# Pooled attention into two MLPs on one core: where weight stores and fetches stand in the order, and the opening of the first block

## The chip, the core and the metric

One core of one Trainium2 chip. The metric is the device time of one execution in microseconds (us). The kernel before took 2052.91 us (median of 3 runs, 2050.61 to 2057.3). TensorE (PE) multiplies, VectorE (DVE), ScalarE (ACT) and GpSimd (POOL) work elementwise, SyncE (SP) issues all the DMAs of this kernel, in program order.

## The reference, cut to what matters

```python
# q, k, v: 8 batches, 8 heads, 576 positions, 64 wide
k_p = k.reshape(B, H, 72, 8, 64).mean(axis=3)       # v_p likewise
scores = (1/8) * q @ k_p^T ;  scores -= max
attn = exp(scores) ; attn /= sum + 1e-9
x = (attn @ v_p) as 4608 tokens x 512
x = (sigmoid(x @ w_gate) * (x @ w_val)) @ w_out     # 512 -> 1536 -> 512
h = x @ w_in                                        # 512 -> 2048
y = where(h > 0, h, exp(min(h, 0)) - 1) @ w_out     # 2048 -> 512
```

The weights come as 64-bit floats, in DRAM read as pairs of 32-bit integers. Each is narrowed to one 32-bit float by four VectorE operations on integers and then kept as two reduced-precision halves, high and low, so that a product is three matmuls (high x high, high x low, low x high).

## The kernel before, in words

**Stages.** The 4608 tokens go in nine blocks of 512, n = 0 to 8. A prelude (0 to 69 us in the profile) does the attention of block 0 and the first conversions of weights. Blocks 0 and 1 (69 to 229, 229 to 376) run the gated MLP plainly, in twelve steps c over the 1536 columns, while the 36 pieces of w_gate, w_val and w_out are converted (block 0, `convert`) and sums of weights are formed and stored (block 1, `form_weights`). Blocks 2 to 8 (376 to 1282) multiply by a Strassen-like scheme: twelve units u, each of seven products k. The second MLP runs from 1282 to 2050.

**What goes on behind the products.** During block n the attention of block n+1 is worked out, at places (u, k) of a table (`thin_plan`, with Q_AT, S_AT, T_AT). The previous block's output is flushed (`flush_one`, L631 and L638) at u = 0. Also the second MLP's weights are converted by the generator `prepared` (L252 on): 16 pieces of w_in, two and two as a pair, then 16 of w_out. For each there is a fetch to a raw tile (`rw`, L124 or L130), a `magnitude` on ScalarE (L268), four VectorE operations (`narrow_1`, `narrow_2`: L105, L109, L115, L119), differences (L305 to L310), a split in halves (ScalarE L273, GpSimd L277) and a store (`wd`, `wod`, L278). `work()` advances the generator by one step, at the places that WORK_AT names for even and odd u.

**What sets the order.** Each engine runs its instructions in program order; the Python order of the calls is that order. The raw tiles have two buffers in rotation, so a fetch waits until the store that last read its buffer has landed. The tiles `rq`, `rkv`, `yo` share rotating row buffers. SP issues in order too: an issue that waits for its data or its buffer holds up every issue behind it. In the prelude a score tile (`ats`, L482), the exponent, the norm (L513 to L521) and the transposes (`att`, L528) follow tile by tile, and `emit_pv` (L552, L559) multiplies by the values.

Of the kernel before, what the change touches and what calls it, by code (L numbers as in the profile page):

```python
# [24 lines left out]
def fused_kernel(  # L25
# [41 lines left out]
    ps = ctx.enter_context(tc.tile_pool(name="ps", bufs=1, space=PSUM))  # L67
# [137 lines left out]
    def convert(n, ahead=2, peek=1):  # L205

        for _ in range(n):
            i = count["one"]
# [18 lines left out]
    def form_weights(cc, i):  # L227


        wa, wb = wg[2 * cc], wg[2 * cc + 1]  # L230
        ra, rb = plain_t().bitcast(F32), plain_t().bitcast(F32)
        lo, hi = slice(0, HW), slice(HW, NW)
        sub = ALU.subtract
        for r, w in ((ra, wa), (rb, wb)):
            nc.vector.tensor_tensor(out=r, in0=f32(flat(w[:, i, 0])), in1=f32(flat(w[:, i, 1])), op=ALU.add)
            yield
        nc.vector.tensor_tensor(out=ra[:, lo], in0=rb[:, lo], in1=ra[:, lo], op=sub)
        nc.vector.tensor_tensor(out=rb[:, lo], in0=rb[:, hi], in1=rb[:, lo], op=sub)
        yield
        split(flat(wb[:, i, 0, 0:SQ]), flat(wb[:, i, 1, 0:SQ]), ra[:, lo])  # L240
        nc.vector.tensor_tensor(out=rb[:, hi], in0=rb[:, hi], in1=ra[:, lo], op=sub)
        nc.vector.tensor_tensor(out=ra[:, hi], in0=rb[:, hi], in1=ra[:, hi], op=sub)
        yield
        two = raw_tile("t32").rearrange("p f w -> p (f w)").rearrange("p (m s f) -> p m s f", m=2, s=2).bitcast(F32R)
        one = plain_t().rearrange("p (s f) -> p s f", s=2).bitcast(F32R)
        split(two[:, :, 0], two[:, :, 1], rb.rearrange("p (m f) -> p m f", m=2))
        nc.sync.dma_start(out=t_dram[2 * cc + i][:, 0:2], in_=f32(two))
        yield
        split(one[:, 0], one[:, 1], ra[:, hi])
        nc.sync.dma_start(out=t_dram[2 * cc + i][:, 2], in_=f32(one))  # L250
        yield

    def prepared():
# [16 lines left out]
        def upper(r, src):  # L270
            d = r.rearrange("p f w -> p (f w)").rearrange("p (s f) -> p s f", s=2).bitcast(F32R)
            d = d[:, :, :src.shape[1]]
            nc.scalar.activation(out=d[:, 0], in_=src, func=AF.Copy)  # L273
            return d

        def lower(d, src, place):
            nc.gpsimd.tensor_tensor(out=d[:, 1], in0=src, in1=f32(d[:, 0]), op=ALU.subtract)  # L277
            nc.sync.dma_start(out=place, in_=f32(d))  # L278

        def both(place, src):  # L280
            d = upper(raw_tile("rs2"), src)
            lower(d, src, place)

        def narrowed(i):
            for half in (narrow_1(tiles[i]), narrow_2(raws[i], tiles[i])):
                for _ in half:
                    yield
# [4 lines left out]

        fetch(0)
        yield
        magnitude(0)
        yield
        for i in range(len(loads)):
            q, second = divmod(i, 2)
            yield from narrowed(i)
            t, r = tiles[i].bitcast(F32), raws[i]  # L300
            if i < C2 and second:
                a, b = tiles.pop(i - 1).bitcast(F32), t
                c = plain_t().bitcast(F32)
                lo, hi = slice(0, 256), slice(256, 512)
                nc.vector.tensor_tensor(out=c[:, hi], in0=b[:, hi], in1=b[:, lo], op=ALU.subtract)  # L305
                nc.vector.tensor_tensor(out=b[:, lo], in0=b[:, lo], in1=a[:, lo], op=ALU.subtract)
                lower(upper(r, t), t, part(q, 1))
                yield
                nc.vector.tensor_tensor(out=c[:, lo], in0=b[:, hi], in1=b[:, lo], op=ALU.subtract)
                nc.vector.tensor_tensor(out=a[:, hi], in0=c[:, lo], in1=a[:, hi], op=ALU.subtract)  # L310
                yield
                both(part(q, 2), c)
                yield
                both(part(q, 3, 1), a[:, hi])
                fetch(i + 1)
                yield
            else:
                d = upper(r, t)
                fetch(i + 1)
                lower(d, t, part(q, second) if i < C2 else wo2_dram[i - C2])  # L320
                yield
            magnitude(i + 1)
            yield

    def background():
        for cc in range(C1 // 2):
            for i in range(2):
                while formed[0] <= cc:
                    yield
                yield from form_weights(cc, i)  # L330
        yield from prepared()

    formed = [0]
# [12 lines left out]
    ps_at = wide.enter_context(tc.tile_pool(name="ps_at", bufs=1, space=PSUM))  # L346
# [76 lines left out]
    def emit_k(b):  # L423

        a = ps_at.tile([P, 2, 512], F32, name="atk", tag="at")
# [40 lines left out]
    def emit_q(t, d=None):  # L466
        r = q_raw.pop(t)
        if d is None:
            a = ps_at.tile([P, 2, 512], F32, name="atq", tag="at")[:, 0, :]
            d = q_tile()  # L470
        else:
            a = ps.tile([P, 512], F32, name="atq0", tag="acc", bufs=4)
# [16 lines left out]
    def off_peak(p, a, n):  # L489
# [3 lines left out]
        mx = at_p.tile([P, n, H // 2], F32, name="mx", tag="mx")  # L493
# [6 lines left out]
    def emit_s(t, p=None):  # L500
        a = ps_at.tile([P, 2, 512], F32, name="ats", tag="at")
        scores(a, t, range(HP), q_t.pop(t))
        p = p_tile() if p is None else p
# [6 lines left out]
    def emit_norm(t, p):  # L510
        p3 = p.rearrange("p (h k) -> p h k", k=SP)
        sm = at_p.tile([P, H], F32, name="sm", tag="sm")
# [3 lines left out]
        pl = at_p.tile([P, HP, WIN], F32, name="pl", tag="pl")  # L516
# [18 lines left out]
    def emit_t(t, spare=False):  # L535
        if spare:
            a = [ps.tile([P, 512], F32, name="att0", tag="acc", bufs=4) for _ in range(2)]
        else:
            both = ps_at.tile([P, 2, 512], F32, name="att", tag="at")
            a = [both[:, 0, :], both[:, 1, :]]  # L540
# [25 lines left out]
    def emit_pv(n):  # L566

        a = ps_at.tile([P, 2, 512], F32, name="atv", tag="at")
        d = [a[:, 0, :], a[:, 1, :]] + [ps.tile([P, NW], F32, name="xv", tag="gv", bufs=2) for _ in range(2)]
# [79 lines left out]
    Q_AT = (1, 4, 7, 9)  # L649
    S_AT = (2, 5, 8, 10)  # L650
    T_AT = (3, 6, 9, 11)
# [23 lines left out]
    with tc.manual_schedule():  # L675
# [38 lines left out]
        qt = spare("qt0")  # L714
        convert(1, 0, 0)
        for c in range(NCH):
            pool_k(0, c)
        emit_k(0)
        open_to(2)
        for i in range(TPW):  # L720
            emit_q(i, qt[:, i])
        convert(1, 0, 0)
        room = [spare("p0"), spare("p1")]
        room = [r.rearrange("p a n -> p (a n)") for r in room]
        ph = [room[t // 3][:, t % 3 * HK:(t % 3 + 1) * HK] for t in range(TPW)]

        def between(t):

            if t == 0:
                convert(1, 1, 0)  # L730
            elif t == 1:
                for c in range(NCH):
                    pool_v(0, c)
            elif t == 2:
# [654 lines left out]
```

## Time and profile before

| | us |
|---|---|
| median of 3 runs | 2052.91 |
| profiled execution, its own time | 2051.42 |
| its span (first to last instruction) | 2049.7 |
| PE busy | 1825.4 (89%) |
| DVE busy | 1099.1 (54%) |
| ACT busy | 854.8 (42%) |
| POOL busy | 631.2 (31%) |
| chain that ended last | PE 63%, DVE 15%, DMA 8%, ACT 5% |

A busy PE is not PE at full speed: the granted clock (PEclk, in shares of 2.4 GHz) has two levels, 1.2 and 2.4 GHz, and a stretch between them shows a mean below 1. Idle time of PE is the stretch less its busy time.

### The profile page before, as it was taken

Reading aid. Unit: us, or ns where it says so; the run is one execution under the profiler, and the core shown is the slowest. Engines: PE = TensorE matmul, PEld = TensorE weight load, DVE = VectorE, ACT = ScalarE, POOL = GpSimd, SP = SyncE. Lnnn points to the kernel's source line nnn. Section 1 sums busy time; section 2 is a strip of 40 time slices with the busy share of each in tenths; the row PEclk is TensorE's granted clock in tenths of the full one; section 3 lists DMA queues with packets and bytes.
Section 4 is the critical chain, followed back from the end, with each engine's and each line's share of the span. In section 5 each row is a group of like instructions: output and inputs, shape, how many; then the busy total and the mean of one; then the engine's idle time right before and its main releaser. Section 6 shows DMA issues by size and latency. Waiting matters only on the chain.

```text
span 2049.7 us, 27976 instructions
## 1 busy us (share of the span) xinstructions
PE 1825.4 (89%) x10212; PEld 1612.1 (79%) x10212; DVE 1099.1 (54%) x2073; ACT 854.8 (42%) x1727; POOL 631.2 (31%) x635
## 2 busy tenths in 40 slices
PE   3577888698889888988999979999999999999999
PEld 2456766587778877877888869899999999999898
DVE  6689455565555655646656546344434444344432
ACT  3344333343344343433434423444444454444443
POOL 2245244332333232323333322222222222222222
PEclk7698998899999998999999989999999999999999
DMA  6454233655654755656656586634334343343521
GB/s 169 129 172 146 96 128 118 211 175 187 210 195 160 235 189 185 198 180 224 197 197 216 175 325 238 246 118 169 110 138 174 108 172 138 117 165 111 189 110 50
DMA packets 150906, 346.82 MB, mean 169 GB/s; under 512 B 47728, under 2 KB 79472, under 8 KB 150768
## 3 DMA queue, kind: packets, MB, share of 16 engines
q1 hardware_dynamic: 150768, 345.02, 49.4%
q8 instruction: 81, 1.33, 0.3%
q14 instruction: 57, 0.47, 0.1%
HBM read 287.31 MB, written 57.67 MB: 168 GB/s over the span
## 4 chain that ended last, share of the span: by engine, by line
PE 63%; DVE 15%; DMA 8%; ACT 5%; issue 4%; SPq 2%; POOL 2%; ACTq 0%; DVEq 0%; POOLq 0%
PE oacc L1266 19%; PE bank L1220 17%; PE pl L1105 12%; PE acc L606 8%; DMA rw<-in_moe_w_out_dram 2%; PE gv L581 2%; DMA wd<-rs 2%; DMA rw<-in_moe_w_in_dram 1%; DVE sg L1142 1%; PE ats L482 1%; DVE vs L438 1%; SPq L638 1%; DMA rkv<-in_k_dram 1%; DMA rkv<-in_v_dram 1%; DVE sm L513 1%
## 5 line engine op out<-in xcount | busy, mean ns | idle before, releaser
L1220 PE MATMUL bank<-form,wr 128*128 128x384 f32 x2016 | 411.0, 338 | 1.0 <-DVE u L1253 0.7
L1220 PEld LDWEIGHTS bank<-form,wr 128*128 128x128 f32 x2016 | 366.5, 188 | 29.1 <-DVE u L1253 1.1
L606 PE MATMUL acc<-g,wos 128*128 128x512 f32 x1152 | 353.8, 403 | 1.3 <-ACT g L92 1.2
L1266 PE MATMUL oacc<-w2o,gc 128*128 128x512 f32 x1080 | 288.9, 393 | 0.4 <-POOL gc L93 0.4
L1266 PEld LDWEIGHTS oacc<-w2o,gc 128*128 128x128 f32 x1080 | 199.6, 187 | 30.4 <-POOL gc L93 0.8
L606 PEld LDWEIGHTS acc<-g,wos 128*128 128x128 f32 x1152 | 195.2, 194 | 15.0 <-ACT g L92 1.7
L93 POOL TENSOR_TENSOR g<-sg,g 128x512 fp32r<-128x512 f32 x108 | 141.2, 1315 | 174.5 <-ACT g L92 172.1
L1105 PE MATMUL pl<-s,wg 128*128 128x256 f32 x1008 | 159.2, 296 | 37.3 <-DVE u L1120 20.0
L93 POOL TENSOR_TENSOR gc<-ea,gc 128x384 fp32r<-128x384 f32 x96 | 98.1, 1022 | 298.1 <-ACT gc L92 295.0
L1105 PEld LDWEIGHTS pl<-s,wg 128*128 128x128 f32 x1008 | 144.6, 197 | 55.9 <-DVE u L1120 29.5
L1105 PE MATMUL pl<-s,tt 128*128 128x256 f32 x1008 | 163.9, 302 | 22.7 <-DVE sg L1132 17.6
L93 POOL TENSOR_TENSOR gc<-pair,gc 128x384 fp32r<-128x384 f32 x96 | 98.1, 1022 | 260.7 <-ACT gc L92 240.2
L1105 PEld LDWEIGHTS pl<-s,tt 128*128 128x128 f32 x1008 | 148.5, 204 | 34.9 <-DVE sg L1132 18.8
L1105 PE MATMUL pl<-a,wg 128*128 128x256 f32 x1008 | 157.2, 294 | 5.9 <-ACT sg L1127 5.8
L1105 PEld LDWEIGHTS pl<-a,wg 128*128 128x128 f32 x1008 | 146.3, 199 | 16.5 <-ACT sg L1127 6.8
L581 PE MATMUL gv<-x,wg 128*128 128x512 f32 x576 | 150.3, 416 | 8.2 <-DVE sg L599 4.4
L1266 PE MATMUL oacc<-w2p,gc 128*128 128x512 f32 x540 | 143.1, 393 | 0.0
L581 PEld LDWEIGHTS gv<-x,wg 128*128 128x128 f32 x576 | 113.6, 201 | 34.6 <-issue 6.2
L92 ACT ACTIVATE g<-sg 128x512 fp32r<-128x512 f32 x108 | 67.8, 628 | 168.5 <-DVE sg L1142 121.2
L1266 PEld LDWEIGHTS oacc<-w2p,gc 128*128 128x128 f32 x540 | 99.8, 187 | 14.8
L528 PE MATMUL att<-ident,p 128*128 128x128 f32 x144 | 27.9, 326 | 87.5 <-POOL p L521 68.7
L277 POOL TENSOR_TENSOR rw<-nt,rw 128x512 fp32r<-128x512 f32 x32 | 43.6, 1364 | 176.0 <-ACT rw L273 176.0
(199 smaller groups left out, 2841.4 us busy)
## 6 DMA issues: line engine op xcount, KB each, us to landing
wr<-wd SPq DMA_DIRECT2D x96, 896.0 KB, 6.4
tt<-td SPq DMA_DIRECT2D x84, 768.0 KB, 4.7
wos<-wd SPq DMA_DIRECT2D x96, 512.0 KB, 5.7
rw<-in_moe_w_out_dram SPq DMA_DIRECT2D x22, 512.0 KB, 4.3
r<-yd SPq DMA_DIRECT2D x24, 384.0 KB, 7.8
out_dram<-po SPq DMA_DIRECT2D x36, 256.0 KB, 2.0
rw<-in_moe_w_in_dram SPq DMA_DIRECT2D x16, 512.0 KB, 6.2
wd<-rw SPq DMA_DIRECT2D x16, 512.0 KB, 3.5
```

Of the source, the lines that this page charges most:

```text
L92: nc.scalar.activation(out=dst_hi, in_=src, func=AF.Copy)
L93: eng.tensor_tensor(out=dst_lo, in0=src, in1=f32(dst_hi), op=ALU.subtract)
L277: nc.gpsimd.tensor_tensor(out=d[:, 1], in0=src, in1=f32(d[:, 0]), op=ALU.subtract)
L438: nc.vector.tensor_reduce(out=t, in_=r.rearrange("p (r d) -> p d r", r=POOL), op=ALU.add, axis=AX.X)
L482: nc.tensor.matmul(a[o:o + n, i // 2, (i % 2) * w:(i % 2 + 1) * w], lhsT=qt[:, j * P + o:j * P + o + n], rhs=kbd[b % 2][:, j * w:(j + 1) * w],
L513: nc.vector.tensor_reduce(out=sm, in_=p3, op=ALU.add, axis=AX.X)
L528: nc.tensor.transpose(a[:, (c % HP) * P:(c % HP + 1) * P], src, ident)
L581: nc.tensor.matmul(d, lhsT=w[:, i, a_w, j], rhs=x[j][:, a_x], start=(j == 0 and a_w == 0 and a_x == 0), stop=(j == KD - 1 and a_w == 1),)
L606: return lambda: nc.tensor.matmul(acc[m], lhsT=w[:, a_w, m * P:(m + 1) * P], rhs=g[:, a_g], start=(c == 0 and a_w == 0 and a_g == 0), stop ...
L1105: nc.tensor.matmul(src, lhsT=w(a_w, j), rhs=f_t[nm][:, j, a_x], start=opens and m == 0, stop=m == 5, skip_group_check=True,)
L1220: nc.tensor.matmul(bank[b ^ flip], lhsT=wp[q][a_w][:, w, j * P:(j + 1) * P], rhs=form_tile(s, a)[j][:, a_x], start=opens and n == 0, stop= ...
L1266: return lambda: nc.tensor.matmul(acc[t + i], lhsT=g[c][:, a_g, i * P:(i + 1) * P], rhs=wo2[2 * q + e][a_w], start=opens and p == 0, stop= ...
```

## The change

No arithmetic is added or taken away. Eight things move:

- `halves`: the store of a converted w_out piece is issued two conversions later (`stores`).
- `form_weights`: the two stores of a unit's sums wait until the third step of the next unit.
- `prepared`: two fetches ahead at the start; a pair takes 17 steps (15 before); each store is issued at least a step after its split; the fetch of the next piece stands three steps ahead of its magnitude, the one after that about six; w_out pieces take six steps, with the fetch three steps ahead (one before).
- WORK_AT, MORE_AT, LAST_AT: 34 steps in a block, which are two pairs; other places.
- the flush at k = 1, 2, 3, 6 of u = 0 (2 to 5 before).
- attention tables: queries at u = 1, 3, 5, 7, scores at 2, 4, 6, 8, transposes at 4, 6, 8, 10; the norm one product earlier; two steps of the keys one product earlier.
- block 1: seven `work` steps per c, three of them in the middle (six at the end before).
- the prelude: PSUM tiles of two banks in four buffers; the scores of tiles 0 to 3 close together, norms and transposes behind; five conversions ahead of `emit_pv(0)` and one behind (six ahead before).

```diff
+    stores = []
     def halves(dst, then=None):
...
             if then:
-                then()
+                stores.append([2, then])
...
+    for q in range(C2 // 2):                      # prepared, one pair
...
+            de = halved(raws[i], tiles[i].bitcast(F32))
+            magnitude(i + 1)
+            yield
+            steps = narrowing(i + 1)
+            next(steps)
+            yield
+            store(de, part(q, 0))
+            yield from steps
...
+            dc = halved(raw_tile("rs2"), c)
+            yield
+            store(do, part(q, 1))
+            yield
+            store(dc, part(q, 2))
+            da = halved(raw_tile("rs2"), a[:, hi])
+            yield
+            fetch(i + 2)
+            yield
+            store(da, part(q, 3, 1))
+            yield
+            yield
+            magnitude(i + 2)
+            fetch(i + 3)
+            yield
...
-        WORK_AT = ((2, 3, 4, 6), (2,))
+        WORK_AT = ((0, 3, 4), (2, 3))
+        FLUSH_AT = (1, 2, 3, 6)
+        MORE_AT = {(0, 5), (1, 4), (10, 1), (11, 1)}
...
         convert(1, 0, 0)
...
+        scored(0)
         convert(1, 0, 0)
...
+        scored(1)
+        scored(2)
+        emit_norm(0, ph[0])
+        scored(3)
...
+        emit_pv(0)
         convert(1)
-        emit_t(TPW - 1, True)
-        convert(1)
-        emit_pv(0)
```

What SP issues in units 7 to 9 of block 3 of the kernel before (`tt`: the sums for the products, `wos`: w_out of the first MLP, `rkv`, `rq`: rows of keys, values and queries, `wd<-`: stores of prepared weights, `rw<-`: fetches):

```order
L278 DMA wd_109<-rw_4312 256x1x512
L392 DMA rkv<-in_v_dram 128x1x512
L278 DMA wd_109<-rs_4673 256x1x512
L810 DMA tt<-td_91 128x1536
L621 DMA wos_4699<-wd_101 128x1024
L278 DMA wd_109<-rs_4710 256x1x256
L124 DMA rw_4714<-in_moe_w_in_dram 128x4x256
L362 DMA rq<-in_q_dram 128x8x64
L810 DMA tt<-td_92 128x1536
L621 DMA wos_4808<-wd_102 128x1024
```

What SP issues from where the fetches of block 3 now stand:

```order
L305 DMA wd_108<-rs_4206 256x1x512
L126 DMA rw_4319<-in_moe_w_in_dram 128x4x256
L445 DMA rkv<-in_v_dram 128x512
L868 DMA tt<-td_88 128x1536
L673 DMA wos_4362<-wd_98 128x1024
L305 DMA wd_108<-rs_4299 256x1x256
L445 DMA rkv<-in_v_dram 128x512
L126 DMA rw_4445<-in_moe_w_in_dram 128x4x256
L868 DMA tt<-td_89 128x1536
L445 DMA rkv<-in_v_dram 128x512
L673 DMA wos_4469<-wd_99 128x1024
L415 DMA rq<-in_q_dram 128x8x64
```

The fetch stood right behind the last store of its pair, and `rq` and the `tt` of the next unit behind it. Now the two fetches stand units earlier, each with a unit's `tt` and `wos` behind it, and no fetch is left at the old place.

What SP issues at the start of block 4 before (`yd`: the previous block's flushed output):

```order
L278 DMA wd_110<-rw_4955 256x1x512
L638 DMA yd_75<-yo 128x384
L638 DMA yd_76<-yo 128x128
L638 DMA yd_75<-yo 128x384
L638 DMA yd_76<-yo 128x128
L278 DMA wd_110<-rs_5347 256x1x512
L638 DMA yd_75<-yo 128x384
L638 DMA yd_76<-yo 128x128
L810 DMA tt<-td_85 128x1536
L638 DMA yd_75<-yo 128x384
L638 DMA yd_76<-yo 128x128
L390 DMA rkv<-in_k_dram 128x512 x2
```

and of the change:

```order
L690 DMA yd_75<-yo 128x384
L690 DMA yd_76<-yo 128x128
L690 DMA yd_75<-yo 128x384
L690 DMA yd_76<-yo 128x128
L690 DMA yd_75<-yo 128x384
L690 DMA yd_76<-yo 128x128
L868 DMA tt<-td_85 128x1536
L443 DMA rkv<-in_k_dram 128x512 x2
L690 DMA yd_75<-yo 128x384
L690 DMA yd_76<-yo 128x128
L415 DMA rq<-in_q_dram 128x8x64
L305 DMA wd_110<-rw_5023 256x1x512
```

The store of prepared weights ahead of the flushes and the one between them are gone from there, and the first two `rkv` rows of keys come ahead of the last flush, while `rq` stands between the second and third row of keys.

What PE does in the prelude before, from the last tile of queries on (`atq`: queries transposed, `ats`: scores, `att`: probabilities transposed, `atv`, `xv`: product with the values):

```order
L474 MATMUL atq_235<-ident,q_143 128x128 x4
L482 MATMUL ats<-kbd_137,qt_187 128x144 x8
L528 MATMUL att_306<-ident,p_245 128x128 x4
L528 MATMUL att_307<-ident,pl 128x128
L482 MATMUL ats<-kbd_137,qt_187 128x144 x4
L528 MATMUL att_343<-ident,p_245 128x128 x4
L528 MATMUL att_344<-ident,pl 128x128
L482 MATMUL ats<-kbd_137,qt_187 128x144 x4
```

and of the change:

```order
L524 MATMUL atq<-ident,q_140 128x128 x16
L532 MATMUL ats<-kbd_134,qt_184 128x144 x16
L578 MATMUL att<-ident,p_185 128x128 x4
L578 MATMUL att<-ident,pl 128x128
L578 MATMUL att<-ident,p_185 128x128 x4
```

All 16 score products are now one row in the program, and the transposes of the four tiles follow one another with no score between.

## Rows read from the trace of the kernel before

**Rows 1.** Stretches by stage: us, busy of each engine, granted clock, DMA.

```profile
0.00:69.00 69.00, 24.43 (x97) 18.79 (x97) 40.02 (x66) 21.36 (x47) 17.10 (x33) 0.73 0.62 168
69.00:229.00 160.00, 123.09 (x550) 97.97 (x551) 134.43 (x179) 74.05 (x130) 75.31 (x58) 0.89 0.44 142
229.00:376.00 147.00, 124.54 (x565) 102.03 (x564) 80.02 (x125) 54.15 (x102) 58.37 (x60) 0.92 0.37 122
376.00:521.00 145.00, 118.26 (x780) 105.03 (x779) 84.18 (x179) 55.09 (x116) 45.76 (x50) 0.92 0.58 191
521.00:927.00 406.00, 350.91 (x2318) 315.25 (x2317) 237.46 (x511) 159.02 (x335) 128.76 (x139) 0.92 0.59 194
927.00:1053.00 126.00, 115.11 (x778) 101.86 (x777) 78.21 (x168) 52.97 (x112) 42.01 (x46) 0.97 0.65 210
1053.00:1167.00 114.00, 109.09 (x740) 97.38 (x739) 68.27 (x153) 49.76 (x97) 34.93 (x33) 1.00 0.61 202
1167.00:1282.00 115.00, 97.38 (x627) 88.37 (x625) 62.52 (x133) 33.66 (x76) 30.09 (x27) 0.91 0.74 268
1282.00:2050.00 768.00, 762.63 (x3769) 685.42 (x3768) 313.99 (x566) 354.76 (x719) 198.85 (x194) 1.00 0.38 141
```

**Rows 2.** Waits of the whole span: us in total, times, longest.

```profile
...
POOL rw L277 <- ACT rw L273: 176.0, 30, 12.7
...
ACT nt L268 <- DMA rw<-in_moe_w_in_dram: 50.3, 8, 9.7
```

**Rows 3.** Timeline, block n=3: start, us, engine, line, [idle before <- releaser].

```profile
...
594.15 0.52 SPq L278 DMA_DIRECT2D wd<-rs  x1
...
602.00 0.38 SPq L124 DMA_DIRECT2D rw<-in_moe_w_in_dram  x1
...
607.12 0.66 ACT L268 ACTIVATE nt<-rw 128x512 f32<-128x512 f32 x1 [9.40 <-DMA rw<-in_moe_w_in_dram]
...
609.93 1.11 PE L528 MATMUL att<-ident,p 128*128 128x128 f32 x4 [7.87 <-POOL p L521]
```

**Rows 4.** Stretches right behind two stalls, columns as in Rows 1.

```profile
609.90:617.00 7.10, 7.07 (x35) 6.51 (x36) 4.71 (x11) 2.56 (x6) 3.99 (x5) 0.64 0.06 21
667.80:674.60 6.80, 5.63 (x24) 5.13 (x24) 1.19 (x3) 1.21 (x3) 0.73 (x1) 0.61 0.99 325
```

**Rows 5.** Timeline, start of block n=4: TensorE.

```profile
...
667.83 1.65 PE L1105 MATMUL pl<-s,tt 128*128 128x256 f32 x6 [4.05 <-DVE sg L1132]
...
675.64 0.98 PE L1105 MATMUL pl<-s,wg 128*128 128x256 f32 x6 [2.15 <-DVE u L1136]
```

**Rows 6.** Waits of block n=8 (1167 to 1282).

```profile
...
ACT nt L268 <- DMA rw<-in_moe_w_out_dram: 28.8, 5, 10.3
```

**Rows 7.** Waits of block n=1 (229 to 376).

```profile
...
PE atq L474 <- DMA rq<-in_q_dram: 13.2, 2, 7.4
```

**Rows 8.** Timeline, end of the prelude.

```profile
...
52.09 0.34 SPq L175 DMA_DIRECT2D wd<-wo  x1
52.53 0.38 SPq L130 DMA_DIRECT2D rw<-in_moe_w_out_dram  x1
...
57.85 0.66 ACT L199 ACTIVATE nt<-rw 128x512 f32<-128x512 f32 x1 [8.84 <-DMA rw<-in_moe_w_out_dram]
...
59.04 3.23 PE L552 MATMUL atv<-pt,vbd 128*128 128x512 f32 x6 [7.00 <-ACT pt L92]
```

**Rows 9.** VectorE by line, block n=0: form, count, busy, mean ns.

```profile
...
L105 DVE TENSOR_SCALAR nt<-nt 128x512 f32<-128x512 f32 x22 | 19.8, 899 | 2.5 <-ACT nt L199 2.5
```

**Rows 10.** Timeline, prelude: one operation alone, and beside GpSimd.

```profile
...
40.35 0.68 DVE L119 SCALAR_TENSOR_TENSOR nt<-rwo,nt 128x512 int32<-128x512 int32 x1
...
50.62 1.44 POOL L93 TENSOR_TENSOR wo<-nt,wo 128x512 fp32r<-128x512 f32 x1
...
50.87 1.75 DVE L119 SCALAR_TENSOR_TENSOR ntr<-rw,ntr 128x512 int32<-128x512 int32 x1
```

**Rows 11.** DMA issues: count, KB each, median us to landing.

```profile
...
tt<-td SPq DMA_DIRECT2D x84, 768.0 KB, 4.7
```

More of the change, by code (lines that the diff above doesn't have):

```diff
@@ L207, in convert @@
         for _ in range(n):
+            for x in stores:
+                x[0] -= 1
+            while stores and stores[0][0] <= 0:
+                stores.pop(0)[1]()
             i = count["one"]
@@ L268, in magnitude, with halved, store, narrowing @@
                 nc.scalar.activation(out=tiles[i].bitcast(F32), in_=raws[i][:, :, 1].bitcast(F32), func=AF.Abs)
[L270 removed]
+        def halved(r, src):
             d = r.rearrange("p f w -> p (f w)").rearrange("p (s f) -> p s f", s=2).bitcast(F32R)
             d = d[:, :, :src.shape[1]]
[L273 removed]
+            split(d[:, 0], d[:, 1], src)
             return d
[L276 to L277 removed]
+        def store(d, place):
             nc.sync.dma_start(out=place, in_=f32(d))
[L280 to L284, printed above, removed]
+        def narrowing(i):
             for half in (narrow_1(tiles[i]), narrow_2(raws[i], tiles[i])):
[L286 to L287 removed]
+                yield from half
                 yield
@@ L291, in part @@
             return w_dram[q][:, :, 2 * n:2 * n + m].rearrange("p s a f -> p s (a f)")
+        sub = ALU.subtract
+        lo, hi = slice(0, 256), slice(256, 512)
         fetch(0)
-        yield
+        fetch(1)
+        for _ in range(3):
+            yield
         magnitude(0)
         yield
[L297 to L321, printed above, removed]
@@ new lines, in prepared @@
+        last = None
+        for i in range(C2, len(loads)):
+            steps = narrowing(i)
+            next(steps)
+            if last is not None:
+                store(last, wo2_dram[i - 1 - C2])
+            yield
+            next(steps)
+            yield
+            next(steps)
+            if last is not None:
+                fetch(i + 1)
+            yield
+            yield from steps
+            last = halved(raws[i], tiles[i].bitcast(F32))
+            yield
+            magnitude(i + 1)
+            yield
@@ L331, in background @@
+        yield
+        yield
+        store(last, wo2_dram[C2 - 1])
+    def background():
+        yield from form_weights()
         yield from prepared()
-    formed = [0]
     working = background()
@@ L423, in emit_k @@
     def emit_k(b):
[L425 removed]
+        a = two_banks("atk")
         flat = a.rearrange("p a n -> p (a n)")
@@ L533, in keep_p, with emit_t @@
         split(hi, lo, a[:, 0:(c1 - c0) * P].rearrange("p (c n) -> p c n", n=P), nc.vector)
[L535 to L540, printed above, removed]
+    def emit_t(t):
+        both = two_banks("att")
+        a = [both[:, 0, :], both[:, 1, :]]
         for c in range(NCH):
@@ L714, in fused_kernel, with scored @@
         qt = spare("qt0")
+        room = [spare("p0"), spare("p1")]
+        room = [r.rearrange("p a n -> p (a n)") for r in room]
+        ph = [room[t // 3][:, t % 3 * HK:(t % 3 + 1) * HK] for t in range(TPW)]
+        def scored(t):
+            emit_s(t, ph[t])
+            emit_exp(ph[t])
         convert(1, 0, 0)
```

178 lines of the change are left out of this document (102 added, 76 removed).

## The prediction

> **What bounds the kernel now.** I read the stretches by stage first, then the waits, then the timeline at the longest waits. In the stretches [rows 1] the reader is to see that the second MLP is no place for a gain: 762.6 of its 768 us are PE's, at full clock. Before it PE idles: 44.6 us of the prelude's 69, 36.9 in block 0, 22.5 in block 1, 26.7 in block 2, 55.1 in blocks 3 to 5, 10.9 in block 6, 4.9 in block 7, 17.6 in block 8 (each the stretch less PE's busy time). Block 7 is the measure: no conversion that waits, 114 us, clock 1.00. Blocks 2 to 5 do the same kind of work in 135 to 145, with more idle and a granted clock of 0.92.
>
> The cause of the idle time shows in one stall of block 3 [rows 3]. SP issues a store of prepared weights at 594.15. The fetch of the next piece takes over the buffer that this store reads, and goes out only at 602.00. ScalarE, which stands in program order at the magnitude of that piece, is released at 607.12 after 9.40 us; a row norm queued behind it on ScalarE then comes late, GpSimd's product behind that, and PE's transposes at 609.93, after 7.87 us. Over the span ScalarE waits eight times for such fetches of w_in, 50.3 us [rows 2].
>
> A stall costs more than its length: in the 7.1 us behind it PE was busy 7.07 at a granted clock of 0.64, a mean between the two levels [rows 4]. At full clock this work had taken 7.07 x 0.64 = 4.5, so 2.6 us more are lost.
>
> **The change part by part.** The sum is made against the profiled execution's 2051.4 us, 1.5 below the median shown.
>
> *Fetches of w_in, blocks 3 to 5.* The fetches are the same 16, the stores too; only places move. From 602.00 to 607.12 a fetch takes 5.1 us; its buffer comes free 7.85 us after the store's issue (594.15 to 602.00) [rows 3]. Together 13 us from that store to the magnitude. In the new order store and fetch are a step apart, and fetch and magnitude three; at 34 steps in a block of some 118 us a step is 3.5 us on average, so about four steps give 14. The wait is covered, narrowly; where the steps stand close together (u = 10 and 11), a residue of 0 to 3 us is left on ScalarE. The second fetch of a pair has twice the distance. Each block loses the 7.9 + 2.6 = 10.5 us of one stall.
>
> *Flush.* At the start of block 4 DVE waits for a row buffer, which the store of an earlier `yo` still holds, and PE stands 4.05 us [rows 5]; in the 6.8 us behind it PE is busy 5.63 at 0.61 [rows 4], so 5.63 x 0.39 = 2.2 more. The fourth flush moves from k = 5 to k = 6 and the third stays two products ahead of it, with no weight store queued between; I take the 6.2 us as gone. What comes next there is the rows of keys: PE's 2.15 us at 675.64 [rows 5] are a wait of DVE's pooling for a load, and in the new order `rq` is queued behind the first two rows of keys and waits for one of their buffers, so the third and fourth cannot come sooner than the first is pooled. I leave 2.7 us a block for that and for the residue above. So 10.5 + 6.2 - 2.7 = 14 a block, 42 for three. The bounds: nothing (each wait replaced by its like), and the stretch brought to block 7's state, 55.1 - 3 x 4.9 + 406 x 0.08 = 73 [rows 1].
>
> *Block 2* has the first two pieces, and two such stalls: 2 x 10.5 = 21; I take 20, since the first magnitude follows its fetch by only three steps there. Bounds: 0, and 26.7 - 4.9 + 145 x 0.08 = 33 [rows 1].
>
> *Block 6* has the flush alone: 6. Bounds 0 and 10.9 - 4.9 + 126 x 0.03 = 10. *Block 7*: 0; it now holds steps of w_out that stood in block 8, and idles so little that the cost is at most its own 4.9 again, or 5 late.
>
> *Block 8* waits five times for w_out, 28.8 us of ScalarE [rows 6]; PE idles 17.6, of which 12.7 above block 7, and the clock of 0.91 costs 115 x 0.09 = 10. The new fetch stands three steps ahead of its magnitude, but the first one of the block is behind a store and close to it. I take half of 23: 11. Bounds 0 and 23.
>
> *Block 1.* PE waits twice for a row of queries, 13.2 us [rows 7]: its load is queued on SP behind stores of weight sums that wait for their split. These stores now are issued a unit later, when their data is there. 13.2 and two times 2.6 of clock are 18; 16 are taken, as the work steps in the middle of c put more of DVE's operations ahead of the gate's product. Bounds 0 and 22.5 + 147 x 0.08 = 34.
>
> *Prelude and block 0.* At 52.09 SP issues a store of w_out that had waited for its split, and only then, at 52.53, the next fetch; ScalarE waits 8.84 for it, and PE starts the values' product at 59.04, 7.00 us late [rows 8]. With the store two conversions later, the fetch goes out ahead of it. A conversion (some 2.2 us of DVE, two operations at about 0.68 and two shorter, [rows 10] for the longer) comes behind `emit_pv(0)` rather than ahead: gained here, paid back in block 0, where DVE is busy 134.4 of 160 us [rows 1]. Three scores in a row let the norms run while PE still scores; the transposes no longer wait tile by tile for DVE, but DVE's work in the prelude is the same, 40 of 69 us, so I put this at 2. Prelude 7 + 2 = 9; block 0, bound by DVE, 2. Bounds: a loss of 5 (the score tiles take DVE ahead of conversions that block 0 needs first) and a gain of 18, twice the wait of 8.84.
>
> Sum: 42 + 20 + 6 + 0 + 11 + 16 + 9 + 2 = 106. From 2051.4 this gives 1945, with the offset to the median 1946 or 1947; I say 1946.
>
> **A rule that speaks against a part of it.** DVE's L119 takes 0.68 us alone at 40.35, but 1.75 at 50.87, where GpSimd had begun a 1.44 us operation at 50.62 [rows 10]. And L105 averages 899 ns over block 0's 22 of that form [rows 9]. By the Trainium skill, SBUF — State Buffer, section Who interferes with whom, a VectorE instruction with two inputs in SBUF and a GpSimd instruction that reads SBUF shut each other out for a whole instruction, whichever starts first. The trace agrees: GpSimd ends at 52.06, 0.68 more is 52.74, and L119 ended at 52.62. By that rule, closing the gaps only makes the two meet more often. What this does here, from rows: block 0 is DVE's, and work that is drawn together in the prelude and block 1 comes back as longer operations. That is the second rival.
>
> **Rivals.**
> 1. *The fetch is still late.* Where the buffer comes free later than 7.85 us after the store, or steps bunch, the stall of 10.5 us stays in blocks 2 to 5 once each, and block 8 keeps its 11: 1946 + 42 + 11 = 1999. For it: the margin is 14 against 13 us. Against it: the new fetch of the second piece has much more room, and the old order had none at all.
> 2. *DVE and GpSimd collide.* Prelude and block 0 gain nothing (11) and block 1 half (8): 1946 + 19 = 1965. For it: 134 of 160 us busy. Against: blocks 1 to 8 keep DVE at 62% or less.
> 3. *It goes further:* the key rows' wait goes too, and the clock stays up: of the upper bounds' sum (73 + 33 + 10 + 23 + 34 + 18 = 191) three quarters, 143: 1909.
> 4. *Slower.* SP is one queue, and a deferred store that waits at its head for GpSimd's low half holds up `tt`, the next unit's weights. GpSimd has waited up to 12.7 us for the high half [rows 2]. Two stores of a pair in a row, 2 x 12.7, and 4.7 to land `tt` [rows 11], less the nine products by which `tt` is issued ahead (a unit is 406 / 36 = 11.3 us, a product a seventh, so 14.5), are 15.6 us of PE, with the clock 18.2 a pair; eight pairs are 146: 1946 + 146 = 2092. It is slower from six pairs of eight on. For it: eight stores a block. Against: each stands a step or more behind its split, where before it stood right at it.
> 5. *The change does not do what it says* (the waits are hidden anyway, time the same): 2051. Against: rows 3 follow the stall through to PE.
>
> **How the numbers follow.** Chances: forecast 0.50, with its own range 1925 to 1968; rival 1 0.17; rival 2 0.13; rival 3 0.14; rival 4 0.04; rival 5 0.02. The range, 1900 to 1995, leaves out half of rival 1 (0.08), rivals 4 and 5 (0.06) and the low end of rival 3 (0.05). A change below 0.3%, 6 us, could not be told from none. Faster: 0.94; same 0.02; slower 0.04.
>
> **What would show it.** In the stretches of the changed kernel, cut where its blocks begin: blocks 3 to 5 at about 121 us each with a clock of 0.96 or more, block 2 at 125, block 8 at 104, block 1 at 131. In the waits: ScalarE's wait for fetches of w_in falls from 50.3 to under 15; PE's wait for `rq` in block 1 is gone; the values' product starts at about 50. Wrong: if `tt` or the rows of keys appear among PE's releasers for more than 4 us a block, rival 1 or 4 is at work; if L105 and L119 grow beyond rows 9 and 10, rival 2. The prediction as a whole fails if blocks 3 to 5 stay at 130 or more, or fall to 114.

## The result and the profile after

The changed kernel took 1949.28 us (median of 4 runs, 1948.39 to 1950.39) against 2051.76 us of the kernel before in the same runs: a ratio of 0.9496, 95% interval 0.9477 to 0.9515. Forecast were 1946 us, in a range of 1900 to 1995.

The stretches by stage of the changed kernel, cut at each block's first product, with the columns of [rows 1] (length, busy time of PE, PEld, DVE, ACT and POOL, granted clock, DMA):

```profile
...
0.00:63.80 63.80, 24.47 (x97) 18.11 (x98) 37.83 (x60) 20.41 (x45) 16.53 (x32) 0.77 0.56 156
63.80:225.30 161.50, 123.63 (x550) 99.15 (x550) 142.17 (x185) 75.21 (x132) 79.27 (x60) 0.88 0.46 150
225.30:358.00 132.70, 122.21 (x566) 100.79 (x567) 78.58 (x125) 52.58 (x103) 55.43 (x60) 0.94 0.42 142
358.00:482.50 124.50, 113.88 (x779) 101.61 (x778) 80.18 (x173) 53.89 (x114) 43.85 (x49) 0.97 0.63 211
482.50:844.90 362.40, 337.43 (x2317) 300.43 (x2316) 241.51 (x511) 160.60 (x334) 130.07 (x139) 0.99 0.66 217
844.90:967.80 122.90, 113.90 (x779) 100.69 (x778) 81.59 (x170) 53.67 (x112) 42.59 (x46) 0.99 0.64 211
967.80:1078.60 110.80, 107.78 (x742) 97.51 (x741) 68.68 (x157) 51.04 (x99) 37.73 (x35) 1.00 0.64 214
1078.60:1179.40 100.80, 92.36 (x626) 84.07 (x624) 64.18 (x134) 35.49 (x76) 30.52 (x26) 0.98 0.86 308
1179.40:1946.80 767.40, 762.53 (x3768) 685.36 (x3768) 313.40 (x565) 355.18 (x719) 199.00 (x194) 1.00 0.39 141
```

Blocks 3 to 5 went from PE busy 351 of 406 at a clock of 0.92 to 337 of 362 at 0.99. Busy time fell too: the same products ran at a mean clock nearer to full. The second MLP is as long as it was.

| | before | after | difference | forecast |
|---|---|---|---|---|
| prelude | 69.4 | 63.8 | -5.6 | -9 |
| block 0 | 159.3 | 161.5 | +2.2 | -2 |
| block 1 | 147.5 | 132.7 | -14.8 | -16 |
| block 2 | 144.8 | 124.5 | -20.3 | -20 |
| blocks 3 to 5 | 405.8 | 362.4 | -43.4 | -42 |
| block 6 | 126.2 | 122.9 | -3.3 | -6 |
| block 7 | 114.3 | 110.8 | -3.5 | 0 |
| block 8 | 115.1 | 100.8 | -14.3 | -11 |
| second MLP | 767.3 | 767.4 | +0.1 | 0 |
| sum | 2049.7 | 1946.8 | -102.9 | -106 |

Waits of the whole span after (us in total, times, longest), which answer to [rows 2]:

```profile
...
DVE ks L469 <- DMA rkv<-in_k_dram: 13.0, 6, 2.7
...
ACT nt L296 <- DMA rw<-in_moe_w_out_dram: 9.9, 6, 3.4
...
ACT nt L296 <- DMA rw<-in_moe_w_in_dram: 6.4, 4, 2.4
```

ScalarE's wait for fetches of w_in fell from 50.3 us to 6.4. The timeline of block 3 shows what stands there now, against [rows 3] (start, length, engine, line; SPq is an issue):

```profile
...
510.78 0.97 SPq L305 DMA_DIRECT2D wd<-rs  x1
518.26 0.39 SPq L126 DMA_DIRECT2D rw<-in_moe_w_in_dram  x1
...
528.38 0.38 SPq L126 DMA_DIRECT2D rw<-in_moe_w_in_dram  x1
```
```profile
...
527.75 0.67 ACT L296 ACTIVATE nt<-rw 128x512 f32<-128x512 f32 x1
...
548.19 0.67 ACT L296 ACTIVATE nt<-rw 128x512 f32<-128x512 f32 x1
...
589.10 0.67 ACT L296 ACTIVATE nt<-rw 128x512 f32<-128x512 f32 x1 [1.50 <-DMA rw<-in_moe_w_in_dram]
```

The buffer still comes free only 7.5 us after the store's issue (510.78 to 518.26), and SP still sits on that fetch. But the magnitude comes 9.5 us behind its fetch, the second 19.8 us behind, and neither has an idle time noted ahead of it. From store to magnitude there are 17 us; 14 were reckoned and 13 needed. In the block's second pair, where the steps stand closer, there are only 11 us (578.07 to 589.10), and 1.5 of wait are left, within the residue of 0 to 3 that the prediction gave.

### The profile page after: what moved, and what is told of

Read it like the earlier page. It is cut to its first block, busy times and chain, and to the rows that moved or that the text cites. A ratio compares the mean times of both kernels' runs of the same rounds, so it can differ in the third digit from the quotient of the medians.

```text
span 1946.8 us, 27943 instructions
## 1 busy us (share of the span) xinstructions
PE 1798.2 (92%) x10212; PEld 1587.7 (82%) x10212; DVE 1108.1 (57%) x2073; ACT 858.1 (44%) x1727; POOL 635.0 (33%) x635
## 4 chain that ended last, share of the span: by engine, by line
PE 71%; DVE 18%; ACT 4%; issue 3%; DMA 3%; POOL 1%; SPq 0%; ACTq 0%; DVEq 0%; POOLq 0%
PE oacc L1327 20%; PE bank L1281 18%; PE pl L1166 15%; PE acc L658 9%; DVE nt L117 2%; PE gv L633 2%; PE ats L532 2%; DVE nt L111 1%; DMA rkv<-in_k_dram 1%; DVE nt L107 1%; DVE vs L491 1%; DVE a L95 1%; DVE ks L469 1%; PE pl L599 1%; DVE sm L563 1%
## 5 line engine op out<-in xcount | busy, mean ns | idle before, releaser
L658 PE MATMUL acc<-g,wos 128*128 128x512 f32 x1152 | 349.5, 399 | 0.9 <-ACT g L94 0.4
L1166 PE MATMUL pl<-s,wg 128*128 128x256 f32 x1008 | 154.7, 290 | 37.7 <-DVE u L1181 27.0
L1166 PE MATMUL pl<-s,tt 128*128 128x256 f32 x1008 | 154.9, 291 | 11.5 <-DVE a L95 4.4
L1166 PEld LDWEIGHTS pl<-s,tt 128*128 128x128 f32 x1008 | 138.8, 192 | 23.4 <-DVE u L1202 4.7
L1166 PEld LDWEIGHTS pl<-a,wg 128*128 128x128 f32 x1008 | 140.9, 192 | 18.3 <-DVE sg L1200 9.1
L1327 PEld LDWEIGHTS oacc<-w2p,gc 128*128 128x128 f32 x540 | 99.8, 187 | 14.8
L1198 POOL TENSOR_TENSOR sg<-sg,u 128x256 f32<-128x256 f32 x42 | 33.6, 801 | 206.2 <-DVE u L1197 187.8
L1294 DVE SCALAR_TENSOR_TENSOR ea<-ea,bank 128x384 f32<-128x384 f32 x48 | 26.7, 555 | 117.0 <-ACT ea L1291 117.0
```

The lines of the kernel that those rows point to most:

```text
L658: return lambda: nc.tensor.matmul(acc[m], lhsT=w[:, a_w, m * P:(m + 1) * P], rhs=g[:, a_g], start=(c == 0 and a_w == 0 and a_g == 0), stop ...
L1166: nc.tensor.matmul(src, lhsT=w(a_w, j), rhs=f_t[nm][:, j, a_x], start=opens and m == 0, stop=m == 5, skip_group_check=True,)
L1198: nc.gpsimd.tensor_tensor(out=c22, in0=c22, in1=u4, op=ALU.mult)
L1294: nc.vector.scalar_tensor_tensor(out=e, in0=e, scalar=-1.0, in1=src, op0=ALU.add, op1=ALU.max)
L1327: return lambda: nc.tensor.matmul(acc[t + i], lhsT=g[c][:, a_g, i * P:(i + 1) * P], rhs=wo2[2 * q + e][a_w], start=opens and p == 0, stop= ...
```

## Experiments

All but the last are the changed kernel with one part altered, timed in 3 rounds against the kernel before (the last in 5). Ratios are to the kernel before; the changed kernel's is 0.9496.

**The fetch close to its magnitude.**

```diff
-            fetch(i + 2)
             yield
             store(da, part(q, 3, 1))
             yield
+            fetch(i + 2)
             yield
             magnitude(i + 2)
```

> The change, with the first fetch of each pair of w_in pieces put back to one step ahead of its magnitude (seven fetches; the stores stay late, the second fetch of a pair stays far ahead). Theory A (the distance of the fetch from its magnitude makes the gain of blocks 2 to 5): a step is some 3 us, the fetch takes 5.1, so ScalarE waits 2 to 4 us at seven magnitudes, PE loses most of it and some clock: 1965 to 1985, blocks 3 to 5 at 127 to 130 each. Theory B (the landing of the store ahead of the fetch made the stall, and with the stores late a fetch may stand close): 1949 to 1956, blocks 3 to 5 at 121 to 122.

Measured: 1947.62 us, ratio 0.9481 (0.9465 to 0.9497); blocks 3 to 5 took 362.2. This is theory B, 1 us below its range. ScalarE's wait for w_in rose a little and did not reach PE:

```profile
...
ACT nt L296 <- DMA rw<-in_moe_w_in_dram: 7.9, 5, 2.1
```
```profile
...
480.10:842.30 362.20, 337.44 (x2317) 300.36 (x2316) 241.18 (x511) 160.23 (x334) 130.13 (x139) 0.99 0.66 217
```

So the fetch need not stand three steps ahead of its magnitude: with the stores late, one step is enough. The edit leaves the steps from the store whose buffer the fetch takes to the magnitude as they were (18.4 and 11.6 us in block 3 here, 17.0 and 11.0 in the change). It therefore says nothing against the 14 us from store to magnitude that the prediction set against 13.

**Stores in the step of their split.**

```diff
             de = halved(raws[i], tiles[i].bitcast(F32))
+            store(de, part(q, 0))
             magnitude(i + 1)
...
             do = halved(raws[i + 1], b)
+            store(do, part(q, 1))
...
             dc = halved(raw_tile("rs2"), c)
+            store(dc, part(q, 2))
             yield
-            store(do, part(q, 1))
             yield
-            store(dc, part(q, 2))
```

> The change, with each store of prepared weights (w_in and w_out) issued in the step of its split again; the fetches stay where the change has them. Theory A (fetch distance): 1949 to 1955, since the fetch is as far ahead as before and its buffer comes free sooner. Theory C (a store that waits on SP for GpSimd's half holds up keys, queries and the weights of the next unit): 1960 to 1985, with waits of PE for tt or of VectorE for rows of keys grown by 2 us or more a block.

Measured: 1966.26 us, ratio 0.9566 (0.9545 to 0.9587), 17 us above the change, as theory C had it. The waits of blocks 3 to 5, of this kernel first and then of the change:

```profile
...
DVE ks L467 <- DMA rkv<-in_k_dram: 20.3, 6, 4.7
...
PE pl L1164 <- DVE u L1195: 13.5, 4, 4.5
...
ACT nt L296 <- DMA rw<-in_moe_w_in_dram: 0.2, 1, 0.2
```

```profile
...
DVE ks L469 <- DMA rkv<-in_k_dram: 6.1, 3, 2.1
...
PE pl L1166 <- DVE u L1197: 5.4, 3, 1.9
...
ACT nt L296 <- DMA rw<-in_moe_w_in_dram: 5.3, 3, 2.4
```

ScalarE no longer waits for fetches at all, yet the kernel is slower. VectorE waits for rows of keys, which stand on SP behind stores that wait for their data, 20.3 us instead of 6.1, and PE behind it 13.5 instead of 5.4. What late stores save here is the queue behind them.

**The old order inside, at the new places, and then at the old places.** The whole generator `prepared` of before was put back; first with the new places and two empty steps a pair, then with the old places and cadence too.

```diff
-    def prepared():      # the new one
+    def prepared():      # that of before
...
-        WORK_AT = ((0, 3, 4), (2, 3))        # second kernel only
+        WORK_AT = ((2, 3, 4, 6), (2,))
```

> The change, with the whole conversion of the second MLP's weights in the old order (one fetch ahead of its magnitude and behind the stores of its pair, stores in the step of the split), two empty steps added to a pair so that the cadence of 17 is kept; work places, flush, attention tables, block 1 and prelude stay new. Theory E (late stores or early fetches, either alone hides the landing; the two kernels that undid one of them stayed within 17 us): with both undone the stalls of 7 to 8 us come back in blocks 2 to 5, and part of block 8's: 1995 to 2020, blocks 3 to 5 at 132 to 136. Rival F (the work places and the tables made the gain, not the order inside): 1950 to 1970, blocks 3 to 5 at 121 to 126.

> The change, with the conversion of the second MLP's weights wholly as before: old order inside, old places, old cadence of 15 steps a pair; flush, attention tables, block 1 and prelude stay new. The old order at the new places gave 2005, with its stalls at rows of keys and no transposes late by 7 us. Theory J: places add nothing, 2000 to 2010. Theory K (order and places together made the stalls at the magnitudes): 2015 to 2035, ScalarE's wait for w_in 45 us or more and PE late by 7 us once a block again.

Measured: 2004.83 us (ratio 0.9762, 0.9737 to 0.9786) and 2000.67 us (0.9753, 0.9736 to 0.9771). About half of the change's gain is gone in both. The time came back at two different waits. PE's waits in blocks 3 to 5, at the new places and then at the old:

```profile
...
PE pl L1143 <- DVE u L1174: 18.9, 6, 4.3
...
PE ats L509 <- ACT qT L930: 3.4, 6, 1.8
```

```profile
...
PE ats L506 <- ACT qT L927: 27.6, 6, 5.3
PE pl L1140 <- DVE u L1171: 15.3, 3, 5.8
```

At the old places the stall of [rows 3] is back, twice a block and 4 to 5 us long; it now catches the scores, whose queries ScalarE copies behind the late magnitude, and not the transposes. At the new places no score or transpose is late by more than 2 us, and the rows of keys (L1174) cost instead. Theory E had the time of the first (2004.8 in 1995 to 2020), but not the place of its stalls. Of the second, theory J had the time (2000 to 2010) and theory K the place, though 4 to 5 us long where it said 7, so that its time was 14 us too high. The background's conversion is not all of the gain: with it wholly old, blocks 3 to 5 took 397.5 (405.8 before the change), block 2 133.9 (144.8) and block 8 105.9 (115.1); the rest is due to the other parts. Block 2 lost nothing by the old order at the new places (124.6 against 124.5), but 14.2 us at the old ones (133.9 against 119.7 in the next experiment).

**The old places with the new order.**

```diff
-        WORK_AT = ((0, 3, 4), (2, 3))
+        WORK_AT = ((2, 3, 4, 6), (2,))
```

> The change, with the even and odd units' work places as before (k = 2, 3, 4, 6 and 2) and the four added ones kept, so that a block still has 34 steps; the new order inside a pair stays. Theory J (the order inside, with late stores and early fetches, is enough): 1947 to 1957, blocks 3 to 5 at 120 to 123. Theory K (the places make magnitudes and norms fall apart, and carry a good part of the gain): 1965 to 1990, blocks 3 to 5 at 125 to 132, with ScalarE's wait for fetches of w_in of 20 us or more.

Measured: 1929.54 us, ratio 0.9401 (0.9387 to 0.9416). Neither theory: 20 us faster than the change. Blocks 3 to 5, stretch and PE's largest wait, which in the change was 12.3 us:

```profile
...
476.20:830.00 353.80, 334.65 (x2316) 298.89 (x2316) 234.22 (x511) 159.94 (x334) 127.44 (x139) 1.00 0.67 222
```
```profile
...
PE pl L1166 <- DVE u L1181: 5.1, 3, 1.7
```

```profile
...
PE pl L1166 <- DVE u L1181: 12.3, 14, 1.4
```

L1181 is VectorE's sum behind the product k = 1. One such place in the change, with the conversion's L117 of the work step at k = 0 ahead of the sum:

```profile
...
561.59 1.47 DVE L117 SCALAR_TENSOR_TENSOR nt<-rw,nt 128x512 int32<-128x512 int32 x1
...
562.98 0.41 DVE L1181 TENSOR_TENSOR u<-u,pl 128x256 f32<-128x256 f32 x1
...
563.44 0.74 PE L1166 MATMUL pl<-s,wg 128*128 128x256 f32 x4 [1.38 <-DVE u L1181]
```

With the old places PE waits so three times rather than fourteen, 7.2 us less, of the 8.6 by which the three blocks are shorter; over the whole span these waits fall from 27.0 us in 30 to 14.3 in 10. VectorE was also busy 234 us rather than 242 for the same operations. So the new order inside is worth some 71 us at the old places (2000.7 less 1929.5; the cadence and the four added work places differ too) and 56 at the new ones (2004.8 less 1949.3), and the new places cost 20.

**The flush at its old products.**

```diff
-        FLUSH_AT = (1, 2, 3, 6)
+        FLUSH_AT = (2, 3, 4, 5)
```

> The change, with the flush at k = 2 to 5 of u = 0 as in the kernel before. Theory A (the place of the flush hides the wait for its row buffer): a stall of about 4 us and its clock come back in blocks 3 to 6, also 2: 1969 to 1980. Theory B (the wait came from the store of prepared weights queued on SP between the flushes, which is gone): 1947 to 1953.

Measured: 1959.7 us, ratio 0.9539 (0.9523 to 0.9556), between the two theories. VectorE's wait for a row buffer of `yo` did not come back; the wait for keys grew, since their loads now stand behind one more flush:

```profile
...
DVE ks L469 <- DMA rkv<-in_k_dram: 23.2, 6, 5.3
...
DVE yo L683 <- DMA yd<-yo: 2.3, 1, 2.3
```

Of the 6.2 us a block that I put on the flush, the place brings 1 to 3 (blocks 2 to 6: 127.3, 122.4, 123.1, 122.6, 126.0). That the `yo` wait stays away without the new places fits theory B's weight store, queued on SP between the flushes. The kernel above with the old order at the new places points the same way: its flush stood at its new products, but a weight store went out on SP just ahead of it (487.12 in block 3, the first `yd` at 487.74), and the `yo` wait was 13.7 us in 6 waits. The store was not moved by itself.

**Block 1 as before, and its stores alone.**

```diff
-            store(t_dram[u][:, 2], one)          # kept until the next unit
+            store(t_dram[u][:, 2], one)
+            kept()                               # issued at once, both kernels
...
-                    work(3)                      # first kernel only
-                    work(4)
+                    work(6)
```

> The change, with block 1 as in the kernel before: the stores of weight sums in the step of their split, six work steps at the end of each c. Theory A (these stores at the head of SP's queue made the rows of queries late): block 1 goes from 132.7 back to about 147, with PE waiting some 13 us for rq: 1962 to 1967. Theory D (the row of queries was late because of the places of the attention's steps, which stay new): 1949 to 1953, without waits for rq.

> The change, with the stores of weight sums of block 1 in the step of their split, but seven work steps per c in two groups as the change has them. Theory G (the six steps in one group put VectorE's scores behind them, as the run with all of block 1 old showed at two transposes; the stores matter little): 1947 to 1952, block 1 at 131 to 135, no transposes late by 6 us. Theory A (the stores at the head of SP's queue): 1958 to 1966, waits for rq of 5 us or more.

Measured: 1960.32 us (0.9542, 0.9525 to 0.956) and 1954.81 us (0.9513, 0.9485 to 0.9542). Block 1 took 139.8 and 135.7, where the unaltered code took 130.3 to 132.7 in the other runs. PE's waits in block 1 of the first:

```profile
...
PE att L579 <- DVE p L546: 12.9, 3, 6.4
...
PE atq L525 <- DMA rq<-in_q_dram: 0.6, 1, 0.6
```

With stores and steps as before, the rows of queries still are not late: 0.6 us instead of 13.2 [rows 7]. What is late are transposes, and the timeline of the first kernel shows two things ahead of their scores on VectorE:

```profile
...
283.91 0.33 SPq L250 DMA_DIRECT2D td<-t  x1
...
285.64 0.59 SPq L446 DMA_DIRECT2D rkv<-in_v_dram  x1
...
290.03 1.01 DVE L492 TENSOR_REDUCE vs<-rkv 128x64 f32<-128x512 f32 x1 [3.68 <-DMA rkv<-in_v_dram]
...
294.53 0.74 DVE L545 TENSOR_REDUCE mx<-ats 128x8 f32<-128x576 f32 x1
...
296.21 1.09 PE L579 MATMUL att<-ident,p 128*128 128x128 f32 x4 [6.09 <-DVE p L546]
```

VectorE first stands 3.68 us for a row of values, which SP issues only behind a store of weight sums (`td<-t`) that waits for GpSimd (95.3 us in ten such waits in this block); then come six work steps, and only then the scores (L545). The stall of 6.42 us has the same two parts. So stores at the head of SP's queue do hold up loads in block 1, but those of values: VectorE's waits for them there were 18.6 us in the kernel before, none in the change, and 7.9 and 5.5 in these two kernels. Issuing the stores a unit later makes SP's own wait at them shorter, but does not end it (104.1 us in ten waits in block 1 before, 76.5 in nine in the change).

The stores alone cost block 1 some 3 to 5 us and block 2 some 4 (128.4 against 124.5). Both times lie between the two theories given for them, and the second kernel's interval overlaps the change's. Block 1's remaining 7.7 (147.5 to 139.8) must come from what the first kernel kept. Of that, the new places of queries, scores and transposes act here (the three tables count the steps c of blocks 0 and 1, not the units of later blocks), and so do the second buffers that the change gives to the tiles `mx`, `sm` and `pl` of scores and norms; none was tried alone.

**The low halves on VectorE.** In `halves` the second half of a split was moved from GpSimd to VectorE, at first in the same place, then four operations later.

```diff
-            split(hi, lo, t.bitcast(F32))
+            split(hi, lo, t.bitcast(F32), nc.vector)     # first kernel
...
+            nc.scalar.activation(out=hi, in_=src, func=AF.Copy)   # second kernel
+            lows_1.append(lambda: nc.vector.tensor_tensor(
+                out=lo, in0=src, in1=f32(hi), op=ALU.subtract))
...
                 for t in turns:
                     next(t, None)
+            low_1()
```

> The change, with the low halves of the 36 converted pieces of the first MLP subtracted on VectorE and not on GpSimd. Theory H (VectorE's conversions are long because GpSimd's subtractions shut it out): 30 of the pieces fall in block 0; VectorE gets 30 x 0.68 = 20 us more operations there, but its four operations of a conversion fall from some 0.9 to 0.41 and 0.68, and block 0 gets shorter by 5 to 15: 1935 to 1945. Rival (they are long for another reason, such as ScalarE or DMA traffic): block 0 gets longer by 10 to 20: 1960 to 1970.

> The change, with the low halves of the first MLP's pieces on VectorE as in the run before this one (there block 0's VectorE was busy 125 us and not 142, but stood some 25 us behind ScalarE's high halves), now placed at the end of the conversion that splits, four operations behind the high half. Theory H (GpSimd's subtractions make VectorE's conversions long; what was lost in the run before was the wait for ScalarE): VectorE's wait for the high halves falls below 8 us, block 0 takes 148 to 156 and the whole 1936 to 1945. Rival (block 0 is bound by PE's own order, 124 us at a low clock): block 0 stays at 159 to 165, the whole 1946 to 1956.

Measured: 1954.75 us (0.9515, 0.949 to 0.9539) and 1931.97 us (0.9418, 0.9401 to 0.9435). VectorE by line in block 0 (count, busy, mean ns, idle before), of the change, the first and the second kernel:

```profile
...
L107 DVE TENSOR_SCALAR nt<-nt 128x512 f32<-128x512 f32 x24 | 23.3, 972 | 3.8 <-ACT nt L203 3.8
L111 DVE TENSOR_SCALAR nt<-nt 128x512 int32<-128x512 int32 x24 | 18.0, 749 | 0.0
```

```profile
...
L95 DVE TENSOR_TENSOR wg<-nt,wg 128x512 fp32r<-128x512 f32 x16 | 11.1, 692 | 11.2 <-ACT wg L94 11.2
...
L107 DVE TENSOR_SCALAR nt<-nt 128x512 f32<-128x512 f32 x24 | 10.3, 428 | 0.0
L111 DVE TENSOR_SCALAR nt<-nt 128x512 int32<-128x512 int32 x24 | 10.0, 417 | 0.0
```

```profile
...
L107 DVE TENSOR_SCALAR nt<-nt 128x512 f32<-128x512 f32 x24 | 12.2, 508 | 0.0
...
L166 DVE TENSOR_TENSOR wg<-nt,wg 128x512 fp32r<-128x512 f32 x16 | 10.9, 682 | 2.7 <-ACT wg L165 2.7
```

and the stretch of block 0 in the first and in the second:

```profile
...
63.80:233.40 169.60, 126.20 (x550) 101.14 (x550) 124.89 (x219) 75.25 (x132) 26.93 (x26) 0.85 0.45 143
```

```profile
...
63.20:208.80 145.60, 122.61 (x550) 98.59 (x550) 124.62 (x219) 74.85 (x132) 33.19 (x26) 0.91 0.51 167
```

L107 falls from 972 to 428 ns, L111 from 749 to 417. VectorE has 34 operations more and is busy 125 us rather than 142. In the first kernel it stands behind ScalarE's high halves (11.2 us at one form alone) and block 0 takes 169.6; with the low halves behind other work it takes 145.6 against 161.5. The operations became short as theory H said, but its times missed: the first kernel lies between the theory and its rival, as the wait for ScalarE takes the gain, and the second is 4 us faster than theory H's range. The change's own trace separates the two cases too: of the 32 operations of L107 in its block 0, the 8 that met no operation of GpSimd took 414 to 423 ns, and the 24 that met one took 1131 on the mean.

**Keys pooled one product later.**

```diff
-                for u, k, c in ((1, 2, 0), (1, 4, 1), ...
+                for u, k, c in ((1, 3, 0), (1, 5, 1), ...
```

> The change, with VectorE's pooling of the first two rows of keys one product later (k = 3 and 5 of u = 1). If the wait of 1.7 to 2.6 us at the start of blocks 2 to 6 is the landing of these rows, it falls by 1.4 us or more each: 1940 to 1946, and VectorE's wait for them falls from 13 us to under 6. Rival (what frees the row buffers moves with it, SP stands longer at rq, and the third row of keys is late in its place): 1948 to 1955.

Measured: 1943.13 us, ratio 0.9461 (0.9435 to 0.9487), which overlaps the change's interval. VectorE's wait for keys was 14.5 us in 13 waits (13.0 in 6 before this edit), the longest 2.0 instead of 2.7. Inconclusive: the time lies in the range of the first theory, but the wait did not fall below 6 us; the waits became shorter and more.

**Both gains together.** The second of the two kernels with low halves on VectorE, with the old places.

> The change, with the two edits that alone gave 1932 (low halves of the first MLP's pieces on VectorE, four operations behind the high halves) and 1929.5 (the work places of before, the order inside a pair as in the change). They act in different blocks (0 against 2 to 7). If the gains add: 1949.3 - 17.3 - 19.7 = 1912, with block 0 at 144 to 148 and blocks 3 to 5 at 116 to 121. If they share a cause (a clock that stays up, or SP's queue): 1920 to 1930.

Measured: 1909.91 us, ratio 0.9299 (0.9284 to 0.9314). The gains add, and this beats both kernels: 7.0% below the one before.

```profile
...
64.40:210.80 146.40, 123.09 (x550) 99.04 (x550) 124.61 (x219) 74.90 (x132) 33.17 (x26) 0.90 0.52 166
462.60:812.70 350.10, 333.23 (x2317) 297.37 (x2316) 234.21 (x511) 159.68 (x334) 127.50 (x139) 1.00 0.68 225
```

## Why the prediction was right, and where its steps were not

The time was 3 us above the forecast and the largest terms came out at their size: blocks 3 to 5 43.4 for 42, block 2 20.3 for 20, block 1 14.8 for 16. What bounded the kernel was read rightly: stalls of PE ahead of the second MLP, and a clock that fell with them. The causes behind three terms were not.

*Fetches.* I said that "the wait is covered, narrowly" by the steps from a store to the magnitude. The rows bear this out: 17 and 11 us with waits of 0 and 1.5, where 13 stood with a wait of 9.4 before. How far the fetch itself stands ahead of the magnitude does not matter, as the first experiment shows. What the term left out is what the stores hold up on SP besides the fetch. Late stores with the close fetch (the second of a pair stayed early) free ScalarE and the rows of keys; early fetches alone free ScalarE, but leave the keys' wait, 17 us. The old order has neither, and 71 us hang on it at the old places; how much of them each part brings was not separated. The sum came out because the stall's length was read from the trace, whatever removes it.

*Places of the work steps.* I priced their move at nothing, and named no work that hid it. It costs 20 us, of which PE's waits for the sum behind k = 1, with a VectorE operation now ahead of it, are some 13. No rival had this. It offsets in part that the order inside is worth more than I gave it.

*Flush and block 1.* The 6.2 us of the flush are not its place's alone, and block 1's rows of queries were not late by its stores alone: with these back, `rq` waits 0.6 us. The mechanism that I named, a load behind a store that waits on SP, was there, but at the rows of values, and it is worth 3 to 5 us of block 1. Its term of 16 was near the measured size, but what brought 7.7 of the 14.8 us was not separated. Blocks 7 and 8 brought 7 us more than forecast; with the old conversion in the old places they take 109.3 and 105.9, so block 7's gain and 9.2 of block 8's 14.3 are not the conversion's, though I put block 8 wholly on the fetches of w_out; which other part it is was not tried.

*Prelude and block 0.* The values' product starts at 50.06, as I said (about 50), and stalls again at 52.94. But the three scores in a row brought little: the first transposes of the four tiles still wait for their norms (4.84, 1.92, 7.29 and 4.72 us), and the first product of block 0 is late by 4.82, where it was 3.37 before. PE's timeline:

```profile
...
42.00 1.11 PE L578 MATMUL att<-ident,p 128*128 128x128 f32 x4 [7.29 <-POOL p L571]
...
52.94 2.50 PE L599 MATMUL atv<-pt,vbd 128*128 128x512 f32 x5 [2.08 <-DVE pt L95]
...
63.82 2.47 PE L633 MATMUL gv<-x,wg 128*128 128x512 f32 x5 [4.82 <-DVE x L95]
```

So of the 9 us by which the values' product starts earlier, 5.6 are left. Block 0 grew by 2.2, with VectorE busy 142.2 rather than 134.4 [rows 1]. It holds two more conversions, not one: the change has four of them ahead of `emit_pv(0)` and not five, where six stood, and L107 runs 32 times in block 0, where L105 ran 30 times. Over prelude and block 0 the same 144 operations of the conversions took 126.4 us rather than 120.4: longer operations, as rival 2 had it. Of its price of 19 it took about 8: prelude and block 0 brought 3.4 rather than 11, while block 1 kept its gain. The two kernels with low halves on VectorE show its mechanism: without GpSimd's subtractions VectorE's operations are short again. By the Trainium skill, SBUF — State Buffer, section Who interferes with whom, whichever of the two engines first takes the ports that they share keeps them for its whole instruction, and the other is blocked. These runs agree: L107 takes 414 to 423 ns alone and 1131 on the mean beside GpSimd. What I did not draw from it is that taking them apart is worth 16 us of block 0 (161.5 to 145.6).

The other rivals: fetches still late (1999) did not come, as ScalarE's 6.4 us show; a queue of stores that makes the change slower did not come either, but the second experiment shows that SP's queue was the right place to look, with keys and not `tt` as the sufferer. The change did not go further (1909) either: the keys' wait stayed. The forecast's remainder of 2.7 us a block was the keys' wait, 1.94, 1.73 and 1.78 us of PE in blocks 3 to 5.

That the total came within 3 us is in part luck: prelude and block 0 fell 7.6 us short and block 6 2.7, blocks 7 and 8 brought 6.8 more, and the 20 us that the new places cost are hidden in terms that came out at their size.

## What to carry to other kernels

Where one queue issues stores and loads in order, put a store behind the work it waits for, and ask what stands behind it in the queue; this mattered more than how early the load was. Price each place to which a background step is moved by what it delays on its own engine, even if the number of steps is the same. Where two engines slow each other's operations, taking work from the one that is not the bottleneck onto the one that is can shorten both, if its inputs are ready by then.

## What was not expected of the hardware

The rule in the prediction spoke of VectorE's operations with two inputs. GpSimd's subtractions lengthened those with one input as well, of which [rows 9] was a sign: L107 averaged 972 ns beside them and 428 without, L111 749 and 417, so that 34 more operations on VectorE came with 17 us less busy time (142.2 to 124.9). The length of block 0, where VectorE is busy 142 of 161 us, also varied with the same code there, from 161.4 to 164.4 us in the profiles of the change and of nine experiments. Blocks 3 to 5, 362.4 us in the change, took 361.0 to 362.7 in the four experiments that left their code alone.
